# A long convolution with a spectral mix on one core: the last batch's output taken from each half block of u, in groups of four positions by 89 rows

## The chip, the core and the metric

The kernel runs on one core of one Trainium2 chip. TensorE (PE) does the matrix products, its weight loads are shown apart as PEld; ScalarE (ACT) and VectorE (DVE) take results out of the matmul accumulator (PSUM); SyncE (SP) issues the stores. The metric is the device time of one execution in microseconds (us). The trace has its own clock, which starts with the span; all times on that clock are given so.

## The reference, cut to what is computed

For x of 8 batches by 5696 positions by 128 channels and a filter h of 5696 by 128:

```python
L = 2 * S
y = np.fft.irfft(np.fft.rfft(x, n=L, axis=1) * np.fft.rfft(h, n=L, axis=0)[None], n=L, axis=1)[:, :S, :]
X = np.fft.rfft(y, axis=1)                 # 64 lowest modes mixed by w_r + i w_i over the channels
Y[:, :64] = X[:, :64] @ (w_r + 1j * w_i)   # per mode; the other modes are zero
u = y + np.fft.irfft(Y, n=S, axis=1)
out = u + np.maximum(u @ w_ch, 0.0)        # 8 x 5696 x 128, float32
```

## The kernel before, in words

A position s is written s = 64 q + p, with 89 values of q and 64 of p (`J = 64`, `NQ = 89`). The transforms are matmuls with constant tables. The batches go in four pairs (`g_` from 0 to 3). A first stage, up to some 250 us, makes spectra and parks them in a scratch tensor of the device memory; a last stage, in which all that follows lies, brings them back (`load_zt`, L503) and makes the output.

The last stage has two kinds of work.

- `u_tile` (L754) makes u for one batch, eight values of p and all 89 q: 2 matmuls of 356 columns and 16 of 89 columns into two PSUM banks, and one evacuation of 712 elements that writes the tile u transposed, 128 channels by 5696 positions. The evacuation goes to ACT in five cases of eight and to DVE in three. A block is 16 values of p (`ZB`), four blocks (`NCH`) make a batch, so a batch has 8 half blocks.
- `o_tile` (L808) makes 512 outputs per row: four matmuls whose weights are 128 positions of u, taken at a step of `NW` = 44, and whose moving operand is the 256 columns of w_ch and the identity, into two PSUM banks; then ACT makes the relu into one of three R buffers, and DVE adds u and writes an O buffer. A batch of 5696 positions has eleven such tiles of 128 rows by 4 positions and a tail of 64 positions. Two tiles share one O buffer of 1024 columns (`NO8` = 7 buffers) and are stored by one DMA of 128 rows by 4 KB; the eleventh and the tail have small buffers and stores of their own (`Os`).

Both kinds take their two banks from the same four places in turn (`LSLOT`, L722). The order of the work is written out by hand at the end of the function: all engines follow the order in which the code records it, and `Recorder` (L21) puts in the waits. `todo` is a list of o_tiles that are due. After each half block of u some of them are taken from its head. A batch's o_tiles read every position of u at a step of 44, so they come due only when all 8 half blocks of the batch are done.

For the last pair the order is batch 0's four blocks, then batch 1's. At its start 24 o_tiles (of pair 2) are due. After each half block of batch 0 two are taken, after the half blocks of batch 1 two and three in turn; the 12 of batch 0 come due in the middle. When the last half block of u is done, three more o_tiles of batch 0 are taken and then the 12 of batch 1, for which no u work is left. In the last batch tiles 8 to 10 are stored singly (256 KB each).

```python
for half in range(2):
    u_tile(i, b, half)
    for _ in range((2, 2 + half)[n >= NCH] if last else 1 + half):
        if todo:
            o_tile(*todo.pop(0))
```

Every store goes out by `dma("sync", ...)` on SP, in the order of recording, with one of 12 semaphores of the ring `o`; a store waits until the store 12 before it on that ring has landed. SP also issues the loads of the parked spectra; those of the last block are issued at 329.54 us, before pair 3 starts. The loads of x at the start of the kernel (`x_load`, L352) are split into 80 and 9 rows (`QA`, L338), with rows of 4 KB that lie 32 KB apart in memory.

Of the kernel before, what the change touches and what calls it, by code (L numbers as in the profile page):

```python
# [4 lines left out]
P = 128  # L5
# [4 lines left out]
ADD = mybir.AluOpType.add  # L10
# [3 lines left out]
RELU = mybir.ActivationFunctionType.Relu  # L14
# [109 lines left out]
def bass_long_conv_fft__then__afno_spectral_mix_kernel(nc, x, h, moe_w_r, moe_w_i, moe_w_ch, out):  # L124
    B, S, D = x.shape
    M = moe_w_r.shape[0]
    assert D == P and M == 64 and B == 8
    J = 64
    NQ = S // J
# [3 lines left out]
    NP = B // 2  # L133
# [72 lines left out]
    def at(name, cols, dt, off):  # L206
        return nc.alloc_sbuf_tensor_at(name, [P, cols], dt, offset=off)
# [45 lines left out]
    ZB = 16  # L253
# [13 lines left out]
    u_sb = [at(f"UT{i}", S, F16, u_off[i]) for i in range(4)]  # L267
# [3 lines left out]
    NO8, NO = len(o_big), len(o_off)  # L271
    o8_sb = [at(f"O{i}", 1024, F32, o_big[i]) for i in range(NO8)]
    o_sb = [at(f"Os{i}", 512, F32, o_off[i]) for i in range(NO)]
    r_off = [a_g + 16384 + 2048 * i for i in range(3)]
    NR = len(r_off)
    r_sb = [at(f"R{i}", 512, F32, r_off[i]) for i in range(NR)]
# [12 lines left out]
    def pv(bank, off, dims, p0=0, n=P):  # L289
        return bass.AP(ps, p0 * 4096 + bank * 512 + off, [[4096, n]] + [list(d) for d in dims])  # L290

    R = Recorder(nc)
# [3 lines left out]
    def bank(i):  # L296
        return ("bank", i)
# [18 lines left out]
    def dma(eng, dst, src, ring, reads=(), writes=(), after=()):  # L316
        R.add(eng, lambda h_: h_.dma_start(dst, src), reads, writes, ring=ring, after=after)  # L317

    def mm(o, l, r, st, sp, reads, writes):
        R.add("tensor", lambda h_: h_.matmul(o, l, r, start=st, stop=sp), reads, writes)  # L320
# [3 lines left out]
    def once(key, toks):  # L324
        if key in first:
            return []
        first[key] = 1
        return list(toks)
# [3 lines left out]
    def turns(name, items):  # L332
        i = ring2.get(name, 0)
        ring2[name] = i + 1
        return items[i % len(items)]


    QA = 80  # L338
# [59 lines left out]
    W1, W2, WI = wc_sb[:, 0:P], wc_sb[:, P:2 * P], wi_sb[:, :]  # L398
# [17 lines left out]
    for j in range(16):  # L416
        t = turns("h", [0, 2, 4])
# [85 lines left out]
    def load_zt(i, eng="sync", more=()):  # L503
        g_, c_ = divmod(i, J // ZB)
        for part, (p0, r0, n) in enumerate(((0, 0, P), (PB, P, RB))):
            old = list(once(("zt", i % NC, part), zt_old[i % NC][part])) + list(more) + pace
            dma(eng, bass.AP(zt[i % NC][part], p0 * ZP, [[ZP, n], [1, ZP]]),
                bass.AP(zs, (g_ * 2 * NK + r0) * J * 256 + c_ * ZB * 256, [[J * 256, n], [1, ZP]]),
                "q" if eng == "gpsimd" else "t", [("zd", g_, s_) for s_ in range(NT)], [("zt", i % NC, part)], after=old)
# [212 lines left out]
    LSLOT = [0, 2, 4, 6]  # L722
    NCH = J // ZB
# [30 lines left out]
    def u_tile(i, b, half):  # L754
        g_, c_ = divmod(i, NCH)
        t = ahead.get((i, b, half))
        if t is None:
            t = u_z(i, b, half)
        else:
            for hb in range(2):  # L760
                u_c(i, b, half, t, hb, False)
        ub = (g_ % 2) * 2 + b
        old = {0: WT, 1: WT, 2: U_ALL, 3: U_ALL}[ub]
        n_ev[0] += 1
        e = "scalar" if n_ev[0] % 8 in (0, 2, 3, 5, 7) else "vector"
        src = pv(t, 0, [[1, NQ], [512, 2], [NQ, 4]])
        evac(bass.AP(u_sb[ub], c_ * ZB + half * 8, [[S, P], [J, NQ], [4, 2], [1, 4]]),
             src, [bank(t), bank(t + 1)], [("u_", ub, 2 * c_ + half)], eng=e, after=once(("u", ub), old))
# [16 lines left out]
    for hb in range(2):  # L785
        evac(bass.AP(y_sb, hb * 32 * B, [[2 * M * B, P], [B, 32], [M * B, 2], [1, B]]),
             pv(6 + hb, 0, [[2 * B, 32], [B, 2], [1, B]]), [bank(6 + hb)], [("y", hb)], eng="vector" if hb else "scalar",
             after=ZY)
    for b in range(B):
        bk = 6 + b // 4  # L790
# [10 lines left out]
    n_o = [0]  # L801
    o_cur = [0]
    o8_old = [H_ALL] * 2 + [U_ALL] + [G_ALL + ZX] * 2 + [WT] * 2
    o_old = [H_ALL] * 2 + [M_ALL[5:6], U_ALL + [("f1",)]]
    NW = S // P
    TAIL = S - NW * P

    def o_tile(g_, b, r4):  # L808
        ub = (g_ % 2) * 2 + b
        bb = 2 * g_ + b  # L810
        t = turns("l", LSLOT)
        i = n_o[0]
        n_o[0] += 1
        full = r4 < NW // 4
        last_ = (g_, b) == (NP - 1, 1)
        wide = r4 < (8 if last_ else NW // 4 // 2 * 2)
        big = wide or (last_ and full)
        h_ = r4 % 2 if wide else 0
        if big:
            if not h_:  # L820
                o_cur[0] = turns("o8", list(range(NO8)))
            ob, key, old = o8_sb[o_cur[0]], ("o8", o_cur[0]), o8_old[o_cur[0]]
        else:
            k_ = turns("os", list(range(NO)))
            ob, key, old = o_sb[k_], ("os", k_), o_old[k_]
        OW = 1024 if big else 512
        n, rows = (4, P) if full else (1, TAIL)
        rd = [("u_", ub, c_) for c_ in range(2 * NCH)] + [("wch",), ("i16",)]
        for j in range(n):
            lh = bass.AP(u_sb[ub], 4 * r4 + j, [[S, P], [NW, P]]) if full else u_sb[ub][:, NW * P:S]  # L830
            mm(pv(t + j // 2, (j % 2) * 256, [[1, 256]], 0, rows), lh, WI, True, True, rd, [bank(t + j // 2)])
        bk = [bank(t), bank(t + 1)] if full else [bank(t)]
        rs = r_sb[i % NR]
        rv = bass.AP(rs, 0, [[512, rows], [P, n], [1, P]])
        ov = bass.AP(ob, h_ * 512, [[OW, rows], [P, n], [1, P]])
        src_r, src_u = pv(t, 0, [[256, n], [1, P]], 0, rows), pv(t, P, [[256, n], [1, P]], 0, rows)
        R.add("scalar", lambda e: e.activation(rv, src_r, RELU), bk, [("r", i % NR)], after=once(("r", i % NR), G_ALL + XTT + [("y", 0), ("y", 1), ("id",)]))  # L837
        R.add("vector", lambda e: e.tensor_tensor(ov, src_u, rv, ADD), bk + [("r", i % NR)],  # L838
              [key + (h_,)], after=once(key, old))
        if wide and not h_:  # L840
            return
        w_ = (2 if wide else 1) * 4 * D
        if full:
            dst = bass.AP(out.tensor, out.offset + bb * S * D + (4 * r4 - 4 * h_) * D, [[NW * D, P], [1, w_]])
            src = ob[:, 0:w_]
        else:
            dst = bass.AP(out.tensor, out.offset + bb * S * D + NW * P * D, [[D, TAIL], [1, D]])
            src = ob[0:TAIL, 0:P]
        dma("sync", dst, src, "o", [key + (v_,) for v_ in range(h_ + 1)])

    todo = []
    NB = NCH * NP
    NW4 = NW // 4 + 1
    for g_ in range(NP):
        last = g_ == NP - 1
        order = [(c_, b) for b in range(2) for c_ in range(NCH)] if last else [(c_, b) for c_ in range(NCH) for b in range(2)]
        for n, (c_, b) in enumerate(order):
            i = NCH * g_ + c_
            for half in range(2):
                u_tile(i, b, half)  # L860
                for _ in range((2, 2 + half)[n >= NCH] if last else 1 + half):
                    if todo:
                        o_tile(*todo.pop(0))
            if b == 1 and i + NC < NB:
                load_zt(i + NC)
            if last and n == NCH - 1:
                todo += [(g_, 0, r4) for r4 in range(NW4)]
        todo += [(g_, b, r4) for b in range(1 if last else 0, 2) for r4 in range(NW4)]
    while todo:
        o_tile(*todo.pop(0))  # L870
    R.add("sync", lambda e: e.nop(), [], [("o8", i, v_) for i in range(NO8) for v_ in range(2)] + [("os", i, 0) for i in range(NO)])

    R.emit()
# [29 lines left out]
```

## Time and profile before

| what | value |
|---|---|
| median of 3 runs | 380.75 us (380.23 to 383.44) |
| the profiled execution's own time | 383.51 us |
| its span, first to last instruction | 381.7 us |
| mean granted TensorE clock | 0.933 |
| busy share of the span: PE, PEld, DVE, ACT | 95%, 73%, 80%, 82% |
| pair 3 begins (first matmul of its first half block) | 334.04 us |
| last half block of u begins | 365.45 us |
| last DVE instruction ends | 376.48 us |

A timeline line has the start, the duration, the engine, the source line, the operation with out<-in and shape, the count of merged instructions, and in brackets the idle time ahead of it with what ended it. All matmuls have line L320 and all DMAs L317, because helpers record them; they are told apart by the tiles: `ps<-IBs,C` opens a half block of u (twice in each), `ps<-WI,UT` are the matmuls of an o_tile, `UT<-ps` is the evacuation of u, `R<-ps` the relu and `O<-ps,R` the sum. In a table of windows each engine has its busy time and its instructions, then come the granted clock, the busy share of the 16 DMA engines and their rate.

### The profile page before, as it was taken

To read this page: it belongs to the slowest core of one execution; us is meant where nothing else is said; L and a number is where in the kernel's file an instruction comes from. 1 tells how busy PE (TensorE), PEld (TensorE's weight loads), DVE (VectorE), ACT (ScalarE), POOL (GpSimd) and SP (SyncE) were. 2 spreads that over 40 slices of the span, in tenths; PEclk is the share of its full clock that TensorE was granted. 3 is DMA by queue.
4 is the path that set the end of the run, shared out by engine and by line. 5 is a ranking of instruction groups with operands and counts; after the bars stand their busy time and mean duration, and the time that the engine had idled before them with its cause. 6 is when DMAs were issued, how large, how long until landed. Compare 5 with 4: busy or idle time off the path is not lost.

```text
span 381.7 us, 11950 instructions
## 1 busy us (share of the span) xinstructions
PE 363.6 (95%) x5107; PEld 280.4 (73%) x5107; DVE 303.7 (80%) x331; ACT 311.9 (82%) x492; POOL 83.9 (22%) x137
## 2 busy tenths in 40 slices
PE   7998989999989999999999899999999999999992
PEld 4898856667856667766668666668898988888871
DVE  7566998998988998889998888766347766777784
ACT  8357989998989998999998899994466777777783
POOL 8400012320823311822203211339000000000000
PEclk9997999999999999999999999996899999999997
DMA  7998589998999996999996599999999999999867
GB/s 137 201 280 349 140 228 227 276 269 238 107 134 228 234 269 167 143 129 250 235 283 119 137 298 251 300 328 406 407 388 402 402 415 414 404 408 378 342 256 313
DMA packets 84560, 103.92 MB, mean 272 GB/s; under 512 B 22126, under 2 KB 68974, under 8 KB 81538
## 3 DMA queue, kind: packets, MB, share of 16 engines
q1 hardware_dynamic: 59643, 67.73, 51.3%
q0 software_dynamic: 24864, 35.43, 44.3%
q8 instruction: 40, 0.66, 0.7%
q14 instruction: 13, 0.11, 0.1%
HBM read 70.61 MB, written 51.12 MB: 319 GB/s over the span
## 4 chain that ended last, share of the span: by engine, by line
PE 82%; ACT 9%; DVE 6%; issue 1%; DMA 0%; DVEq 0%
PE ps L320 82%; ACT As L310 7%; DVE As L314 2%; DVE U L597 1%; DVE Hs L312 1%; ACT R L837 0%; DMA F<-cF 0%; DVE UT L312 0%; ACT UT L308 0%; ACT XT L310 0%; DVE O L838 0%; PE ps L791 0%; ACT Hs L308 0%; DVE Os L838 0%; ACT Ah L310 0%
## 5 line engine op out<-in xcount | busy, mean ns | idle before, releaser
L320 PE MATMUL ps<-U,Wc 128*128 128x512 f16 (+1 forms) x368 | 95.8, 384 | 0.0
L605 DVE TENSOR_TENSOR U<-Xs,Hs 128x2048 f16<-128x2048 f16 (+1 forms) x68 | 80.7, 1189 | 11.5 <-ACT Xs L308 10.0
L308 ACT CAST Xs<-ps 128x1024 f16<-128x1024 f32 (+1 forms) x72 | 69.5, 971 | 7.8 <-PE ps L320 4.8
L838 DVE TENSOR_TENSOR O<-ps,R 128x512 f32<-128x512 f32 x81 | 52.5, 686 | 19.8 <-ACT R L837 12.5
L308 ACT CAST Zs<-ps 128x512 f16<-128x512 f32 (+1 forms) x126 | 66.0, 604 | 0.0
L837 ACT ACTIVATE R<-ps 128x512 f32<-128x512 f32 x96 | 50.9, 573 | 14.6 <-PE ps L320 14.1
L314 DVE TENSOR_SCALAR As<-ps 128x720 f16<-128x720 f32 (+1 forms) x60 | 50.1, 879 | 9.1 <-PE ps L320 8.0
L310 ACT ACTIVATE As<-ps 128x720 f16<-128x720 f32 (+1 forms) x72 | 51.6, 772 | 6.6 <-PE ps L320 5.7
L320 PE MATMUL ps<-F,Xin 128*128 128x180 f16 x512 | 54.5, 255 | 2.6 <-ACT Ah L310 1.0
L320 PEld LDWEIGHTS ps<-F,Xin 128*128 128x128 f16 x512 | 46.8, 156 | 9.3 <-DVE As L314 2.6
L320 PE MATMUL ps<-WI,UT 128*128 128x256 f16 x360 | 52.5, 281 | 0.5 <-DVE O L838 0.4
L320 PE MATMUL ps<-As,M 64*128 64x128 f16 x1440 | 48.9, 217 | 4.3 <-DVE U L597 3.5
L320 PEld LDWEIGHTS ps<-U,Wc 128*128 128x128 f16 x368 | 28.5, 98 | 28.5 <-ACT Zs L308 6.1
L320 PEld LDWEIGHTS ps<-As,M 64*128 64x128 f16 x1440 | 40.5, 94 | 10.9 <-DVE U L597 4.2
L317 POOL DMA_DIRECT2D Xt<-in_x_dram x48 | 24.8, 520 | 102.9 <-PE ps L320 102.2
L605 DVE TENSOR_TENSOR U<-ps,Hs 128x2048 f16<-128x2048 f32 x20 | 45.7, 2283 | 0.0
L308 ACT CAST UT<-ps 128x712 f16<-128x712 f32 x40 | 30.0, 752 | 18.7 <-PE ps L320 18.7
L320 PEld LDWEIGHTS ps<-WI,UT 128*128 128x128 f16 x360 | 39.5, 152 | 4.4 <-issue 2.2
L320 PE MATMUL ps<-IBs,C 128*128 128x356 f16 x128 | 40.8, 328 | 0.4
L320 PEld LDWEIGHTS ps<-G,Zs 128*128 128x128 f16 x492 | 27.3, 97 | 13.3
L308 ACT CAST Zt<-ps 128x512 f16<-128x512 f32 (+1 forms) x58 | 31.0, 606 | 0.1
L320 PE MATMUL ps<-G,Zs 128*128 128x2 f16 (+2 forms) x492 | 30.5, 192 | 0.0
(88 smaller groups left out, 500.3 us busy)
## 6 DMA issues: line engine op xcount, KB each, us to landing
out_dram<-O SPq DMA_DIRECT2D x39, 512.0 KB, 10.4
zscr<-Zs SPq DMA_DIRECT2D x60, 256.0 KB, 6.3
Xt<-in_x_dram POOLq DMA_DIRECT2D x24, 320.0 KB, 6.9
zscr<-Zt SPq DMA_DIRECT2D x28, 256.0 KB, 6.6
W<-wscr POOLq DMA_DIRECT2D x8, 512.0 KB, 5.3
M<-cM POOLq DMA_DIRECT2D x5, 720.0 KB, 20.3
ZT0a<-zscr SPq DMA_DIRECT2D x3, 1024.0 KB, 13.4
Xr<-in_x_dram POOLq DMA_DIRECT2D x8, 320.0 KB, 13.8
```

What stands on the lines that cost most here:

```text
L308: R.add(e, lambda h_: h_.copy(dst, src), reads, writes, after=after)
L310: R.add(e, lambda h_: h_.activation(dst, src, COPY, scale=scale), reads, writes, after=after)
L312: R.add(e, lambda h_: h_.tensor_copy(dst, src), reads, writes, after=after)
L314: R.add(e, lambda h_: h_.tensor_scalar_mul(dst, src, scale), reads, writes, after=after)
L317: R.add(eng, lambda h_: h_.dma_start(dst, src), reads, writes, ring=ring, after=after)
L320: R.add("tensor", lambda h_: h_.matmul(o, l, r, start=st, stop=sp), reads, writes)
L597: R.add("vector", lambda e, b=b, s_=s_: e.tensor_tensor(bass.AP(u_s[i], b * 512, [[2048, P], [1024, 2], [1, n * D]]), s_, hv, MULT), [tok, ...
L605: R.add("vector", lambda e: e.tensor_tensor(uv, src, hv, MULT), bk + [("h", t, 0), ("h", t, 1, 0), ("h", t, 1, J)], [("u", i)])
L837: R.add("scalar", lambda e: e.activation(rv, src_r, RELU), bk, [("r", i % NR)], after=once(("r", i % NR), G_ALL + XTT + [("y", 0), ("y", 1 ...
L838: R.add("vector", lambda e: e.tensor_tensor(ov, src_u, rv, ADD), bk + [("r", i % NR)], [key + (h_,)], after=once(key, old))
```

## The change

The last batch (batch 1 of pair 3) no longer uses `o_tile`. Each half block of its u yields two new tiles, recorded by `o_last`: tile i takes the four positions p0+4i to p0+4i+3 and, as weights, the 89 values of q at a step of 64, so it reads that half block alone. It has the same four matmuls of 256 columns, the same relu of 512 columns and the same sum, on 89 rows in place of 128. The two tiles of a half block fill one O buffer, which goes out in two stores: 80 rows and 9 rows of 4 KB, 32 KB apart in the output. The last batch so has 16 tiles and 16 stores, where it had 12 tiles and 8 stores.

The order changes with it: three tiles are taken after every half block of pair 3, four after each half of its last block. The 24 tiles of pair 2 are all taken during batch 0's half blocks, batch 0's own 12 during the first two blocks of batch 1, and the new tiles from then on. After the last half block of u six tiles are left, all of the new kind.

```diff
-        last_ = (g_, b) == (NP - 1, 1)
-        wide = r4 < (8 if last_ else NW // 4 // 2 * 2)
-        big = wide or (last_ and full)
+        big = wide = r4 < NW // 4 // 2 * 2
...
+    def o_last(c_, half, i):
+        ub, bb, p0 = 2 * ((NP - 1) % 2) + 1, B - 1, c_ * ZB + half * 8
+        t = turns("l", LSLOT)
+        k_ = n_o[0]
+        n_o[0] += 1
+        if not i:
+            o_cur[0] = turns("o8", list(range(NO8)))
+        ob, key, old = o8_sb[o_cur[0]], ("o8", o_cur[0]), o8_old[o_cur[0]]
+        for j in range(4):
+            mm(pv(t + j // 2, (j % 2) * 256, [[1, 256]], 0, NQ), bass.AP(u_sb[ub], p0 + 4 * i + j, [[S, P], [J, NQ]]), WI, True, True,
+               [("u_", ub, 2 * c_ + half), ("wch",), ("i16",)], [bank(t + j // 2)])
+        bk = [bank(t), bank(t + 1)]
+        rv = bass.AP(r_sb[k_ % NR], 0, [[512, NQ], [P, 4], [1, P]])
+        ov = bass.AP(ob, i * 512, [[1024, NQ], [P, 4], [1, P]])
+        src_r, src_u = pv(t, 0, [[256, 4], [1, P]], 0, NQ), pv(t, P, [[256, 4], [1, P]], 0, NQ)
+        R.add("scalar", lambda e: e.activation(rv, src_r, RELU), bk, [("r", k_ % NR)])
+        R.add("vector", lambda e: e.tensor_tensor(ov, src_u, rv, ADD), bk + [("r", k_ % NR)], [key + (i,)], after=once(key, old))
+        if i:
+            for q0, n in ((0, QA), (QA, NQ - QA)):
+                dma("sync", bass.AP(out.tensor, out.offset + (bb * S + p0 + q0 * J) * D, [[J * D, n], [1, 8 * D]]), ob[q0:q0 + n, :], "o",
+                    [key + (v_,) for v_ in range(2)])
+
+    def o_next():
+        e = todo.pop(0)
+        (o_last if e[0] == "q" else o_tile)(*e[e[0] == "q":])
...
-                for _ in range((2, 2 + half)[n >= NCH] if last else 1 + half):
+                for _ in range(3 + (n == 2 * NCH - 1) if last else 1 + half):
                     if todo:
-                        o_tile(*todo.pop(0))
+                        o_next()
+                if last and b:
+                    todo += [("q", c_, half, v_) for v_ in range(2)]
...
-        todo += [(g_, b, r4) for b in range(1 if last else 0, 2) for r4 in range(NW4)]
+        if not last:
+            todo += [(g_, b, r4) for b in range(2) for r4 in range(NW4)]
     while todo:
-        o_tile(*todo.pop(0))
+        o_next()
```

## The prediction

> **What bounds the kernel now.** I read the table of windows over the last pair first, cut at the begin of the pair, of its second batch, of the last half block of u, of the first tile after it, and at the last DVE instruction.
>
> ```profile
> core 0: us, PE busy (x) PEld busy (x) DVE busy (x) ACT busy (x) POOL busy (x), PEclk, DMA share, GB/s
> 334.04:349.78 15.74, 15.73 (x205) 13.67 (x206) 11.85 (x19) 11.42 (x23) 0.00 (x0) 0.95 0.97 396
> 349.78:365.45 15.67, 15.52 (x192) 13.30 (x192) 12.60 (x20) 11.48 (x22) 0.00 (x0) 0.95 0.82 328
> 365.45:368.84 3.39, 2.94 (x33) 2.27 (x32) 2.13 (x4) 2.94 (x8) 0.00 (x0) 0.95 0.74 302
> 368.84:376.49 7.65, 6.00 (x41) 4.45 (x41) 7.59 (x14) 6.48 (x12) 0.00 (x0) 0.95 0.76 301
> 376.49:381.70 5.21, 0.00 (x0) 0.00 (x0) 0.00 (x0) 0.00 (x0) 0.00 (x0) 0.60 0.73 283
> ```
>
> Three things stand here. Up to 365 PE is full and DVE and ACT have room (12.60 and 11.48 of 15.67). From 368.84 it is DVE that is full (7.59 of 7.65). Then nothing computes for 5.21 us, and only stores drain. The DMA engines, full at the start (0.97), have room from 350 on. Bytes: 396 x 15.74 + 328 x 15.67 + 302 x 3.39 + 301 x 7.65 + 283 x 5.21 make 16.2 MB after 334.04. Four batches of 2.92 MB and the last small stores of pair 1 (0.29 MB) are 11.95, so some 4.2 MB were queued at 334.04.
>
> Next the timeline of PE and of DVE, for the price of a half block of u with its o_tiles.
>
> ```profile
> 360.76 0.32 PE L320 MATMUL ps<-IBs,C 128*128 128x356 f16 x1
> 361.75 1.71 PE L320 MATMUL ps<-WI,UT 128*128 128x256 f16 x12
> 363.54 0.33 PE L320 MATMUL ps<-IBs,C 128*128 128x356 f16 x1
> 364.53 1.08 PE L320 MATMUL ps<-WI,UT 128*128 128x256 f16 x8
> 365.45 0.32 PE L320 MATMUL ps<-IBs,C 128*128 128x356 f16 x1
> ```
>
> ```profile
> 362.59 0.89 DVE L312 CAST UT<-ps 128x712 f16<-128x712 f32 x1
> 363.39 1.88 DVE L838 TENSOR_TENSOR O<-ps,R 128x512 f32<-128x512 f32 x3
> 369.50 6.80 DVE L838 TENSOR_TENSOR O<-ps,R 128x512 f32<-128x512 f32 x11
> 376.21 0.27 DVE L838 TENSOR_TENSOR Os<-ps,R 64x128 f32<-64x128 f32 x1
> ```
>
> From one opening matmul to the next is a half block: with two tiles 1.91 (363.54 to 365.45), of which u takes 0.99 and 8 matmuls 0.92, so 0.115 each. With three tiles 2.78 (360.76 to 363.54) where DVE evacuates u in it; the same view gives 2.60 for another such (356.25 to 358.85, a tail among its tiles) and 2.47 where ACT does it (351.68 to 354.15). The eleven sums of the last batch run one after the other, 0.62 each.
>
> Last the stores: SP's timeline at the end, and the landing of stores on a quiet ring (window 362 to 366).
>
> ```profile
> 371.95 6.19 SPq L317 DMA_DIRECT2D out_dram<-O  x7
> 378.19 0.65 SPq L317 DMA_DIRECT2D out_dram<-Os  x1
> ```
>
> ```profile
> out_dram<-O SPq DMA_DIRECT2D x2, 512.0 KB, 2.9
> ```
>
> The last store is issued at 378.19, 1.7 us after DVE is done, because SP is still issuing the earlier ones; it lands 3.1 later (same view, window 374 to 379), at 381.3, and the span ends 0.4 after that. A quiet store of 524 KB takes 2.9; at some 410 GB/s 1.3 of it is moving, so 1.6 is fixed.
>
> **The change, part by part.**
>
> *Work added.* 64 matmuls in place of 45 for the last batch: 19 x 0.115 = 2.2 us of PE. Relus and sums: 16 of 512 columns in place of 11 and a tail: ACT 5 x 0.557 (6.68 us for 12 in the tail) less 0.27, 2.5; DVE 5 x 0.62 less 0.27, 2.8. That a sum has 89 rows in place of 128 I count as no saving: the columns are the same.
>
> *The weight load at a step of 64.* No row has this step. 128 columns at a step of 130 paced the matmuls of Xin at 106 ns (54.5 us for 512 of 180 columns), 64 columns at that step those of Hp at 60 ns (15.4 us for 256 of 90 columns): 0.83 to 0.94 ns a column, so 89 columns take 74 to 84, hidden by the 115 of the matmul ahead. I take nothing; it costs from 115 ns up (rival E). A gain there is excluded, since the 256 columns pace the matmul.
>
> *Order.* The instruction order of the changed kernel shows six tiles after the last half block of u, where 15 stood. All 16 half blocks carry three tiles or four. Of the 14 with three, six have u on DVE (the choice counts evacuations and does not change): 8 x 2.47 + 6 x 2.69 = 35.9, less 0.6 for two tails not in those rows; two with four at 2.47 + 4 x 0.115 = 2.93. The last half block so begins at 334.04 + 35.3 + 2.9 = 372.3 (365.45 now). Behind it ACT is the limit: evacuation 1.19 after the begin, 0.65, six relus at 0.557, one sum of 0.69: the last sum ends at 378.2, where it is 376.48 now. If every half block went at 2.47 it is 376.9. The tail of 12 tiles at DVE's pace is gone, but its work and 4 tiles more now stretch the half blocks.
>
> *Waits for buffers.* Pair 2's stores come faster onto a ring with 4.2 MB queued. A store issued at 334 to 338 lands 12.6 later by the landing view; an O buffer comes round after seven pairs, about 16.8 tiles, so 16 us at two tiles per 1.91 and 13.9 at three per 2.5, less 1.2 for filling. Price: nothing to 1 us on DVE around 346 to 350. It moves the engines' end, not the stores', as the ring stays full meanwhile; I take nothing.
>
> *The stores.* SP issues 16 for the batch in place of 8; a store took 0.33 to 1.14 to issue here, the latter where the ring was full. Two per pair of tiles fit into the 1.3 to 1.7 us between pairs. The ring's semaphores make a store wait for the one twelve earlier, six pairs or some 9 us back, against 4.7 to land: no wait. What decides is how fast 80 and 9 rows move. No store here has fewer rows than 128, tails aside. The nearest row is the load of x and h at the start, 80 and 9 rows as well, with the same 32 KB between rows; by bytes these fill the ring until 24 us:
>
> ```profile
> 12.00:15.00 3.00, 3.00 (x40) 2.40 (x38) 2.95 (x5) 0.66 (x1) 2.08 (x4) 0.95 1.05 208
> 15.00:18.00 3.00, 3.00 (x56) 3.00 (x56) 2.31 (x4) 1.65 (x3) 0.00 (x0) 0.95 1.10 217
> 18.00:24.00 6.00, 6.00 (x106) 6.00 (x105) 3.40 (x6) 3.29 (x5) 0.00 (x0) 0.95 1.05 211
> ```
>
> The DMA engines are full and move 211 GB/s, half of the 396 to 415 of 128-row traffic. At 211 a pair of tiles (364,544 bytes) takes 1.73 us; at 410 0.89. These are the bounds; I take 1.73, because shape and pitch are the same. Loads are not stores and POOL issued them, so it is a near row, no proof.
>
> The Trainium skill, "SBUF — State Buffer", section "Door 1: The DMA port swizzle", says that partitions 0 to 63 reach only 8 of 16 ports, about 218 GB/s, no more than 32 partitions do. The 208 to 217 above agree in size. By the page alone the first 64 rows take 1.20 us per pair, and by that estimate the stores would keep up with the tiles and the sum would be that of rival B.
>
> *Sum.* All bytes but the last batch's, 13.3 MB at 410, leave the ring at 366.4. The first new pair is ready 3.8 after the begin of the 13th half block (3.8 as from 363.54 to the second sum's end at 367.37): 366.9 to 368.0. I take 367.0, as the ring will hardly be idle before. Then 8 x 1.73 = 13.8, fixed 1.6, end 0.4: 382.8, against a span of 381.7: +1.1. The profiled execution took 383.51, 1.8 more than its span, and lies 2.76 over the median of the three; by its own time the sum is 384.6, carried to the median 380.75 + 1.1 = 381.9.
>
> **Rivals.**
>
> *B, the stores keep up.* If a pair takes under about 1.3 us, the engines decide: last sum 378.2, 0.45 to issue two stores, 2.9, 0.4: 381.9; with 2.47 throughout and 2.6, the shortest landing here, 380.4. Change +0.25 to -1.35, time 379.4 to 381.0, middle 380.4. For it: 410 GB/s elsewhere. Against: 211 for this shape.
>
> *C, the engines mesh better than the rows.* PE alone needs 0.98 + 12 x 0.115 = 2.36 for three tiles; with that the last sum ends near 375.8, the span at 379.2, time 378.2. Against: no three-tile half block went below 2.47.
>
> *D, slower: the new stores fall well below 211.* Between 58 and 61 us, with x loads beside other traffic, the windows show 58, 115 and 158 GB/s at shares of 0.75 to 0.92. At 137 a pair takes 2.66, the span ends at 367.0 + 21.3 + 2.0 = 390.3, time 389.3. It is slower by over 1% from 2.1 us per pair (174 GB/s). Against: those windows hold small packets too.
>
> *E, the step of 64 slows the weight load.* At twice its price, 160 ns, PE gets 64 x 0.045 = 2.9 us longer: last sum 381.1, span 384.8, time 383.9; over 1% from some 180 ns.
>
> That the change does not do what it says is excluded by the instruction order.
>
> **How the numbers follow.** A (stores at 211) 0.45, own range 381.0 to 383.2; B 0.33; C 0.06; D 0.10; E 0.06. The likeliest is A: 381.9. The range takes in A, B, C and the near part of E, 378.2 to 384.8, and leaves out D and the far part of E. A measurement tells about 1% (3.8 us) from no change; A, B and C lie within it. Faster by over 1% has what lies beyond C, 0.03; slower D and most of E, 0.14; within 0.83.
>
> **What would show it.** In the profile after: the last half block of u begins near 372.3 and the last sum ends near 378.2; six tiles lie behind it. The DMA share is near 1 at about 211 GB/s from 367 to the end, with landings growing from pair to pair; landings that stay at 3 to 4 say B. Weight loads of 89 columns with WI matmuls at 0.115 speak against E. Three-tile half blocks much over 2.7, or DVE waiting on stores around 348, would show the sum of the half blocks wrong.

## The result and the profile after

The changed kernel takes 384.17 us (median of 14 runs, 382.52 to 385.81), the kernel before 380.59 (14 runs, 379.15 to 383.44): ratio 1.0092, 95% interval 1.0069 to 1.0115. That is 3.5 us more, clear of noise; the middle of the interval lies just inside the 1% that the prediction called no change, its upper end beyond it.

The profiled execution of the changed kernel has a span of 381.1 us, shorter than the 381.7 of before. The two must not be set against each other as a whole: pair 3 begins at 331.28 in it and at 334.04 in that of before, though nothing ahead of it was changed. Over all profiled executions below the begin lies anywhere from 330.39 to 334.21. So I count from the begin of pair 3: the last sum ends after 45.96 us (before 42.44) and the span after 49.82 (before 47.66).

The end of the changed kernel on PE and on DVE, from their timelines:

```profile
364.49 0.32 PE L320 MATMUL ps<-IBs,C 128*128 128x356 f16 x1
365.47 2.08 PE L320 MATMUL ps<-WI,UT 128*89 128x256 f16 x12
367.39 0.31 PE L320 MATMUL ps<-IBs,C 128*128 128x356 f16 x1
368.37 2.69 PE L320 MATMUL ps<-WI,UT 128*89 128x256 f16 x16
370.90 0.32 PE L320 MATMUL ps<-IBs,C 128*128 128x356 f16 x1
371.88 3.94 PE L320 MATMUL ps<-WI,UT 128*89 128x256 f16 x24
```

```profile
367.04 1.93 DVE L865 TENSOR_TENSOR O<-ps,R 89x512 f32<-89x512 f32 x3 [0.18 <-ACT R L864]
369.93 2.55 DVE L865 TENSOR_TENSOR O<-ps,R 89x512 f32<-89x512 f32 x4 [0.96 <-ACT R L864]
373.44 3.80 DVE L865 TENSOR_TENSOR O<-ps,R 89x512 f32<-89x512 f32 x6 [0.96 <-ACT R L864]
```

The twelve matmuls from 365.47 end at the next opening one at 367.39: 1.92, so 0.160 us each, and sixteen from 368.37 to 370.90 are 0.158 each. The half block with four tiles takes 3.51 (367.39 to 370.90): 0.98 for u and 2.53 for these sixteen, with no wait of PE in it. The number of sums after the last half block is six, and they run at 0.62 as before: a sum of 89 rows is not shorter than one of 128.

The end of the stores (SP's timeline, and the landing in the window 377.4 to 380):

```profile
365.48 12.51 SPq L317 DMA_DIRECT2D out_dram<-O  x16
```

```profile
out_dram<-O SPq DMA_DIRECT2D x1, 320.0 KB, 3.2
out_dram<-O SPq DMA_DIRECT2D x1, 36.0 KB
```

```profile
366.00:369.00 3.00, 3.00 (x33) 2.88 (x32) 2.79 (x5) 2.21 (x4) 0.00 (x0) 1.00 0.62 182
369.00:372.00 3.00, 3.00 (x33) 2.88 (x33) 2.07 (x4) 2.62 (x5) 0.00 (x0) 1.00 0.63 199
377.24:378.50 1.26, 0.00 (x0) 0.00 (x0) 0.00 (x0) 0.00 (x0) 0.00 (x0) 0.98 0.87 270
```

The last windows (rate in the last column, DMA share ahead of it) show the ring with room while the new stores go out, 0.62 and 0.63. The landings stay at 2.7 to 3.2 in all such windows from 364 on: the stores keep up with the tiles. What follows the last sum, the drain, is 3.86 us, where it was 5.22.

### The profile page after: what moved, and what is told of

Read it like the earlier page. It is cut to its first block, busy times and chain, and to the rows that moved or that the text cites. A ratio compares the mean times of both kernels' runs of the same rounds, so it can differ in the third digit from the quotient of the medians.

```text
span 381.1 us, 12009 instructions
## 1 busy us (share of the span) xinstructions
PE 363.9 (95%) x5126; PEld 282.6 (74%) x5126; DVE 306.0 (80%) x335; ACT 313.9 (82%) x496; POOL 84.4 (22%) x137
## 4 chain that ended last, share of the span: by engine, by line
PE 77%; ACT 11%; DVE 7%; DMA 3%; issue 1%; POOL 0%; DVEq 0%
PE ps L320 77%; ACT As L310 7%; DVE As L314 3%; DMA Xt<-in_x_dram 2%; ACT UT L308 1%; DVE U L597 1%; ACT R L835 1%; DVE Hs L312 1%; DVE O L836 1%; DVE UT L312 1%; ACT R L864 0%; DMA F<-cF 0%; ACT XT L310 0%; DVE O L865 0%; DVE U L605 0%
## 5 line engine op out<-in xcount | busy, mean ns | idle before, releaser
L320 PE MATMUL ps<-U,Wc 128*128 128x512 f16 (+1 forms) x368 | 94.4, 376 | 0.3 <-DVE U L605 0.3
L836 DVE TENSOR_TENSOR O<-ps,R 128x512 f32<-128x512 f32 x70 | 45.5, 686 | 17.0 <-ACT R L835 9.8
L320 PE MATMUL ps<-WI,UT 128*128 128x256 f16 (+1 forms) x379 | 55.8, 286 | 0.0
L320 PE MATMUL ps<-F,Xin 128*128 128x180 f16 x512 | 52.8, 250 | 2.8 <-ACT Ah L310 1.0
L835 ACT ACTIVATE R<-ps 128x512 f32<-128x512 f32 x84 | 44.0, 574 | 13.3 <-PE ps L320 13.3
L320 PEld LDWEIGHTS ps<-F,Xin 128*128 128x128 f16 x512 | 45.1, 155 | 9.6 <-DVE As L314 2.7
L320 PEld LDWEIGHTS ps<-WI,UT 128*128 128x128 f16 (+1 forms) x379 | 44.5, 168 | 2.6 <-issue 1.9
```

## The experiments

Ratios are to the kernel before, with 95% intervals. "Last sum" and "end" are counted from the begin of pair 3 in each profiled execution. The difference of two of these ratios has an error of about 0.003, or 1.1 us (0.004 where e1 is one of the two).

| kernel | ratio | last sum | end |
|---|---|---|---|
| before | 1 | 42.44 | 47.66 |
| changed | 1.0092 (1.0069 to 1.0115) | 45.96 | 49.82 |
| e1_contiguous | 1.0088 (1.0054 to 1.0123) | 46.53 | 50.51 |
| e3_order_only | 1.0003 (0.9979 to 1.0027) | 44.94 | 48.40 |
| e4_more_buffers | 1.0057 (1.0037 to 1.0077) | 46.00 | 49.89 |
| e5_order_buffers | 0.9977 (0.9959 to 0.9995) | 43.54 | 47.01 |
| e6_contiguous_buffers | 1.0055 (1.0032 to 1.0078) | 45.15 | 49.24 |
| e7_twelve_tiles | 1.0005 (0.9987 to 1.0024) | 42.89 | 47.42 |
| e8_small_stores_only | 1.0001 (0.9984 to 1.0019) | 45.13 | 47.37 |
| e9_order_spread | 0.9979 (0.9963 to 0.9996) | 42.20 | 46.20 |

The theory after the first look was W: the weight loads, at 0.160 in place of 0.115, cost 64 x 0.045 = 2.9 us, nearly the whole loss. The rivals were the stores (S) and the denser order (O).

**e1_contiguous**: only the last batch's u is laid down with q inside, so that the weights lie side by side.

```diff
+        if (g_, b) == (NP - 1, 1):
+            src = pv(t, 0, [[512, 2], [1, 4 * NQ]])
+            dst = bass.AP(u_sb[ub], (c_ * ZB + half * 8) * NQ, [[S, P], [4 * NQ, 2], [1, 4 * NQ]])
...
-            mm(..., bass.AP(u_sb[ub], p0 + 4 * i + j, [[S, P], [J, NQ]]), WI, ...)
+            mm(..., bass.AP(u_sb[ub], (p0 + 4 * i + j) * NQ, [[S, P], [1, NQ]]), WI, ...)
```

> The changed kernel with one thing undone: for the last batch u is laid down with its 89 values of q side by side, so the new tiles read their weights at a step of 1 in place of 64. Tiles, order and stores stay. Theory W (the weight load at a step of 64 paces the new tiles: 0.160 us per matmul in the trace after, 0.112 for 128 columns at a step of 44): the 64 matmuls go back to about 0.11, PE gets 64 x 0.047 = 3.0 us shorter, the ratio to before falls from 1.009 to 1.000 to 1.003. Theory N (it is the number of weight columns, 89 in place of 128): nothing changes, 1.009. Theory S (the stores of 80 and 9 rows set the end): the matmuls get shorter but the ratio stays at 1.007 or more.

The loads became quick, and the time did not follow. PE's timeline of this run:

```profile
363.10 1.48 PE L320 MATMUL ps<-WI,UT 128*89 128x256 f16 x12
364.41 0.31 PE L320 MATMUL ps<-IBs,C 128*128 128x356 f16 x1
368.37 1.93 PE L320 MATMUL ps<-WI,UT 128*89 128x256 f16 x16
370.74 0.31 PE L320 MATMUL ps<-IBs,C 128*128 128x356 f16 x1 [0.43 <-DVE O L868]
```

Twelve matmuls take 1.31 (363.10 to 364.41), 0.109 each. But the half block with four tiles now ends in a wait for DVE: PE stands 0.43 us until a sum gives back its place in PSUM, and that half block still takes 3.36 us, where it took 3.51. Most of what PE gained there, it waits. N falls, as the matmuls got shorter with 89 columns as before, and W falls as the cause of the whole time. The numbers are those that S forecast; whether the stores are the reason is tested in e8. The same trace had something that was not looked for, on DVE:

```profile
344.42 1.93 DVE L839 TENSOR_TENSOR O<-ps,R 128x512 f32<-128x512 f32 x3 [1.72 <-DMA out_dram<-O]
```

DVE waits 1.72 us until a store has landed and its O buffer is free, and 0.99 at 336 in the same way (put down to PE there; the trace of e3 names the store for both). That is the wait that the prediction priced at up to 1 us and took as nothing. The profiled execution of the changed kernel does not have it, so the last sums of these two traces (46.53 and 45.96) don't show what the loads are worth; e4 and e6 below do.

**e2_bench**: the changed kernel with matmul groups and store groups behind it, nothing taken out.

> The changed kernel with a measurement behind it, so its time is longer by the added part. First groups of 24 matmuls with weights from a finished u tile, n columns at a step of s, with 64 moving columns (128 at 44 and 1; 89 at 44, 1, 8, 16, 32, 62, 63, 64; 64 at 44 and 64) and with 256 (89 at 1, 44, 63, 64; 128 at 44); then groups of eight stores of 4 KB rows into scratch memory: 128 rows at 22 KB pitch, 128 at 32 KB, 80 and 9 at 32 KB, 80 alone, 64 from partition 0, 64 from partition 32. W: 89 columns at 64 take about 160 ns whatever moves, and 63 or 62 about half of that, under the 0.11 of 256 columns. N: all groups of 89 columns take 160 at 256 moving columns, whatever the step. If steps of 8 to 32 are slow too, the cost goes with powers of two. Stores: if the 211 GB/s of the x loads holds for stores, 80 and 9 rows take 1.73 us a pair, 128 rows 1.25 to 1.3 us each; if the rate goes with the ports, 64 rows from partition 32 are faster than 64 from 0.

Times from the start of a group's 24 matmuls to the next marker, per matmul, with 64 moving columns. The granted clock was 0.50 in these groups, except the first (128 at 44: 0.63) and 89 at 44 (0.92):

| columns, step | ns | columns, step | ns |
|---|---|---|---|
| 128, 44 | 62 | 89, 32 | 148 |
| 128, 1 | 54 | 89, 62 | 156 |
| 89, 1 | 76 | 89, 63 | 152 |
| 89, 44 | 163 | 89, 64 | 147 |
| 89, 8 | 160 | 64, 44 | 129 |
| 89, 16 | 162 | 64, 64 | 116 |

The step of 64 is nothing special: 89 columns cost some 150 to 160 ns at every step measured but 1, so W's forecast for 62 and 63 failed, and 128 columns at a step of 44 cost no more than 62. What makes the new load slow is that it is strided and has fewer than 128 columns, both together. With 256 moving columns, at a clock of 1.00, it is 167 (89 at 44), 157 (89 at 63), 154 (89 at 64) and 109 (128 at 44). The group of 89 at 1 with 256 moving columns came out at 200, at a clock of 0.54, so it can't be set beside these; at a clock of 1.00 the same matmul takes 0.109 us in e1, which N did not allow. The Trainium skill, "TensorE: Matmul & The Clock Gate", section "Weight-path perf modes — Fast Weight Load (FWL) and DoubleRow", says that the quick load is on only when there are 128 weights; 109 against 167 at the same step and clock agrees. The Trainium skill, same page, section "LDWEIGHTS (loading the stationary operand)", prices a load at columns / 1.2 ns, an estimate of 74 ns for 89; that agrees with 76 at a step of 1, and not with the strided rows.

The stores in windows inside each group (128 rows at 22 KB pitch, 128 at 32 KB, 80 and 9, 80, 64 from partition 0, 64 from partition 32):

```profile
383.00:391.00 8.00, 8.00 (x60) 7.58 (x61) 0.00 (x0) 0.00 (x0) 0.00 (x0) 0.64 1.03 419
394.00:403.00 9.00, 9.00 (x57) 8.63 (x57) 0.00 (x0) 0.00 (x0) 0.00 (x0) 0.50 1.03 416
407.00:416.00 9.00, 9.00 (x60) 8.23 (x59) 0.00 (x0) 0.00 (x0) 0.00 (x0) 0.50 0.81 254
422.00:428.00 6.00, 6.00 (x33) 5.70 (x32) 0.00 (x0) 0.00 (x0) 0.00 (x0) 0.65 0.96 267
433.00:440.00 7.00, 7.00 (x49) 6.87 (x49) 0.00 (x0) 0.00 (x0) 0.00 (x0) 1.00 0.98 210
444.50:449.00 4.50, 0.00 (x0) 0.00 (x0) 0.00 (x0) 0.00 (x0) 0.00 (x0) 0.74 1.00 409
```

A pitch of 32 KB costs no more than one of 22 KB (416 and 419). The rows' place decides: 64 rows from partition 0 go at 210 GB/s, 64 from partition 32 at 409. The rule on ports that the prediction took from the Trainium skill, "SBUF — State Buffer", section "Door 1: The DMA port swizzle", holds for stores, by these two rows. A pair of 80 and 9 rows goes at 254: 364,544 bytes in 1.43 us, between the 0.89 and the 1.73 of the prediction. As the DMA share is 0.81 in that window, 1.43 is what a pair takes at most.

**e3_order_only**: the kernel before with the new numbers of tiles per half block; the last batch keeps its tiles.

```diff
-                for _ in range((2, 2 + half)[n >= NCH] if last else 1 + half):
+                for _ in range(3 + (n == 2 * NCH - 1) if last else 1 + half):
```

> The kernel before with the new numbers alone: three tiles after each half block of pair 3, four in its last block. The last batch keeps its 128-row tiles and stores, which all lie behind its last half block, as before; four half blocks then have no tile. Theory W: this part costs nothing; 36 tiles in twelve half blocks of 2.55, four half blocks of 1.0 and 12 tiles of 0.62 end some 0.9 us earlier than before: ratio 0.996 to 1.000. Theory O (denser half blocks stall on buffers and engines and that is the loss): 1.004 or more.

1.0003: neither 0.9 us faster nor slower than can be told. The trace has the same waits as e1 (waits from 329 to 352):

```profile
DVE O L838 <- DMA out_dram<-O: 2.8, 2, 1.7
```

So the order would gain about a microsecond and loses it at O buffers whose stores have not landed. That theory (B) and its rival (R), that the wait only moves on, went into the next three.

**e4_more_buffers, e5_order_buffers, e6_contiguous_buffers**: four more O buffers during pair 3, in the place of a scratch load that pair 3 does not use; on the changed kernel, on e3 and on e1.

```diff
+    NX = len(o_big)
+    o_big += [a_as1 + 4 * ZP + 4096 * i for i in range(4)]
...
+        if last:
+            o_turn[:] = ["o8x", list(range(NX, NO8)) + [(ring2["o8"] + k_) % NX for k_ in range(NX)]]
```

> The changed kernel with four more O buffers during pair 3, in the place of a scratch load that pair 3 does not use: eleven in place of seven. Theory B (at three tiles per half block a buffer comes round before its store has landed, and DVE waits: 2.7 us in two waits in the trace of the contiguous variant, 2.8 in that of the order alone): the waits go, the ratio to before falls from 1.009 to 1.002 to 1.006. Theory R (the ring is full then anyway, so the wait only moves to another place): 1.008 or more.

> The order alone, as before, with the four more O buffers. Theory B: the 2.8 us of waits go and the half blocks run at 2.3 to 2.6, so the ratio falls from 1.000 to 0.992 to 0.997, which would be faster than both kernels. Theory R: 1.000, with the time lost at another wait.

> The contiguous variant with the four more O buffers. Theory B: 1.009 falls to 1.001 to 1.004; from this to 1 is what four more tiles on ACT and DVE cost (some 2.4 us) less the shorter drain of the stores. If it stays some 0.8 us under the run with more buffers and a step of 64, that is the part of the weight load that lies on the path.

B holds: 1.0092 to 1.0057, 1.0003 to 0.9977, 1.0088 to 1.0055: 1.0 to 1.3 us each. Each of these steps is about as large as its error, the three together are clear of it. In e5's trace the sums that had waited for stores wait only for ACT and PE:

```profile
335.28 1.89 DVE L841 TENSOR_TENSOR O<-ps,R 128x512 f32<-128x512 f32 x3 [0.65 <-ACT R L840]
343.07 1.89 DVE L841 TENSOR_TENSOR O<-ps,R 128x512 f32<-128x512 f32 x3 [1.21 <-PE ps L322]
```

DVE stands idle at these sums without a late store too, 0.65 and 1.21 us, so 2.7 us of waits cost less than 2.7. The traces of e3 and e5 begin pair 3 at the same time (330.40 and 330.39), and there the last sum comes 1.4 us earlier with the buffers.

The changed kernel's own profiled execution had no such wait, and its time, 382.88, lies 1.3 us under its median. That its other runs have it is what the step from 1.0092 to 1.0057 says; on its own trace it is not shown, and the begin of pair 3, which moves by 3.8 us, could put one run that far under the median as well. e5 is faster than the kernel before by 0.2% and than the changed one by 1.1%, but missed its 0.992 to 0.997, as e6 missed its 1.001 to 1.004.

e4 and e6 differ by the layout of the last batch's u alone (its evacuations take 0.75 us on ACT and 0.89 on DVE in both), and by 0.0002 in ratio: the times can't tell nothing from about 1 us. Their traces, neither of which has a wait for a store, show where the loads matter. These are half blocks 13 to 15 of pair 3 and the stretch from the opening of the 16th to the last sum, in us:

| trace | 13, three tiles | 14, three tiles | 15, four tiles | 16, to the last sum |
|---|---|---|---|---|
| e4, step of 64 | 2.91 | 2.90 | 3.51 | 6.35 |
| e6, contiguous | 2.31 | 2.97 | 3.35 | 6.18 |

The quick loads gain 0.6 us in one half block and little or nothing in the others, 0.85 in all, where 64 x 0.045 = 2.9 had been reckoned. In half block 14 of e6, where DVE evacuates u, twelve quick matmuls still come to 1.92 (365.06 to 366.98), and at the end of 15 PE waits for DVE:

```profile
364.01 0.31 PE L322 MATMUL ps<-IBs,C 128*128 128x356 f16 x1
365.06 1.80 PE L322 MATMUL ps<-WI,UT 128*89 128x256 f16 x12
366.98 0.32 PE L322 MATMUL ps<-IBs,C 128*128 128x356 f16 x1
370.33 0.31 PE L322 MATMUL ps<-IBs,C 128*128 128x356 f16 x1 [0.43 <-DVE O L871]
```

What is left of e6, 1.0055, is the new form of the last batch. Two kernels took it apart.

**e7_twelve_tiles**: e6 with four of the sixteen tiles left out; the stores stay sixteen.

```diff
-        if i:
+        if i or c_ < 2:
...
-                for _ in range(3 + (n == 2 * NCH - 1) if last else 1 + half):
+                for _ in range(3 + (n == 2 * NCH - 1) - (NCH <= n < NCH + 2) if last else 1 + half):
...
-                    todo += [("q", c_, half, v_) for v_ in range(2)]
+                    todo += [("q", c_, half, v_) for v_ in range(1 if c_ < 2 else 2)]
```

> The contiguous variant with more buffers, with the number of the last batch's tiles put back from 16 to 12: in the first four half blocks of that batch the second tile is left out (those positions of the output get old buffer contents; the stores keep their size), and two tiles in place of three are taken in the half blocks of the first two blocks, so that six are still left at the end. Theory T (the four more tiles on ACT and DVE are the price of the change): four half blocks get 0.47 to 0.6 us shorter each, the ratio falls from 1.0055 to 0.999 to 1.001. Theory S (the stores of 80 and 9 rows, or the six last tiles with their drain, are the price): it stays at 1.004 or more.

1.0005, as T said, so the four tiles cost 1.9 us (0.0050 x 380.5, with an error of 1.1). In the traces the four half blocks that lost a tile take 7.86 us in place of 10.13. A tile left out takes its work from PE, ACT and DVE alike, so this run does not say which engine's work it is that pays.

**e8_small_stores_only**: e6 without the stores of 80 rows.

```diff
-            for q0, n in ((0, QA), (QA, NQ - QA)):
+            for q0, n in ((QA, NQ - QA),):
```

> The contiguous variant with more buffers, without the eight stores of 80 rows (most of the last batch's output is left out; the stores of 9 rows stay, so each step of SP keeps its place). Theory S: the stores at 265 GB/s hold up the end; without them the drain falls from 4.1 us after the last sum to about 3 and the ratio from 1.0055 to 1.002 or less. Theory T: only the last store's own moving time goes, 0.5 to 1 us, ratio 1.003 to 1.004.

1.0001, 2.05 us less, as S said and more than T allowed. The trace shows where: the last sum stays (45.13 against 45.15), and from there to the end it is 2.24 us in place of 4.09. The last sums of e6 and of e8 (spans 380.6 and 378.3):

```profile
372.84 3.67 DVE L871 TENSOR_TENSOR O<-ps,R 89x512 f32<-89x512 f32 x6 [0.87 <-PE ps L322]
372.38 3.68 DVE L871 TENSOR_TENSOR O<-ps,R 89x512 f32<-89x512 f32 x6 [0.86 <-PE ps L322]
```

So the stores cost behind the last sum and nowhere ahead of it. Any kernel has to move a last pair, some 0.9 us at 410 GB/s; about 1.1 us of the 2.05 is then the low rate and the queue of the last pairs. That split is worked out, not measured.

**e9_order_spread**: e5 with batch 0's tiles spread over all half blocks of batch 1.

```diff
-                for _ in range(3 + (n == 2 * NCH - 1) if last else 1 + half):
+                for _ in range((3, 1 + half)[n >= NCH] if last else 1 + half):
```

> The order alone with more buffers, but the last pair's first batch spread over the second batch's half blocks: three tiles after each half block of batch 0, then one and two in turn. No half block of u is then without tiles. If the empty half blocks of the order variant cost something (DVE stood 3.3 us there), the ratio falls from 0.998 to 0.993 to 0.997; if PE sets the pace anyway it stays at 0.998.

0.9979, as e5, so the gain to 0.993 to 0.997 did not come. In the trace the last sum comes 1.3 us earlier, and 0.5 of it is given back behind it (4.00 after the last sum against 3.47); the 0.8 us that is left does not show in the times. Both beat the kernel before, by little more than their error, and the changed one.

## Why the prediction was right or wrong, point by point

- *The sum, 381.9.* Measured 384.17: in the range, 2.3 above the sum and above A's own 381.0 to 383.2, and within 1% as forecast. The range and the "within 1%" held by luck as much as by reckoning: the mechanism that was called likeliest, A, was wrong, and the time nearest to the measured one, the 383.9 of rival E, was got from a cost of which only a part came.
- *A: "At 211 a pair of tiles takes 1.73 us ... I take 1.73", and stores that set the end from 367 on.* Wrong. A pair takes 1.43 at most in the bench. The last batch's eight pairs became ready between the first store at 365.5 and the last sum at 377.2, one per 1.7 us on average, the DMA share was 0.62 and 0.63 in place of near 1, and landings did not grow. Rival B was right that the engines decide, not on its time of 380.4. Only the drain pays: e8 says up to 2.05 us, all of it behind the last sum.
- *The weight load, "74 to 84, hidden by the 115 of the matmul ahead. I take nothing."* Wrong: 0.160 per matmul, the very figure of rival E. The rows of Xin and Hp were read as prices of one load per column, at any number of columns; the bench has 62 for 128 columns at a step of 44 and 116 to 129 for 64 columns at 44 and 64. Why Hp's matmuls came every 60 ns is not shown: they write two halves of the output's partitions in turn (the code sets J * r), and a load lasts 214 ns there, so loads overlap, but no run has such pairs, or the step of 130, by itself. E's 2.9 us did not come either: between e4 and e6 it is 0.1 us in the times and 0.85 in the traces, as the engines hand on through the same places in PSUM.
- *The last sum at 44.2 after the begin* (378.2 less 334.04). Measured 45.96. The fourteen half blocks of three took 36.1 (331.28 to 367.39) against 35.3, the four-tile one 3.51 against 2.93, the stretch behind the last opening 6.34 against 5.9. In the trace of the changed kernel the slow loads make 0.5 of the first (e6 takes 35.6) and pace the whole 3.51. "2.47 + 4 x 0.115" would have failed with quick loads as well: e6 takes 3.35, and PE waits there for one of the four places in PSUM, which u and four tiles more than fill.
- *"Waits for buffers ... I take nothing."* Priced too low: 1.0 to 1.3 us in the times, 1.4 at the last sum between e3 and e5. Of the two waits in e1's and e3's traces the later lies 14 us after the begin, in the stretch that was named (346 to 350, 12 to 16 after it), the earlier 6.6 after it, which was not foreseen. The argument that it "moves the engines' end, not the stores'" fell with the stores as the bound.
- *Work added.* ACT 2.5 and DVE 2.8 were worked out for 16 tiles in place of 12; e7 measures 1.9 for four tiles. This was the largest sure loss, and the sum of A did not hold it, as the stores were to set the end.
- *The tail.* Six tiles in place of 15 behind the last half block, and a drain of 3.86 in place of 5.22. The gain is that of the order, not of the new tiles: e3, with the order alone, drains in 3.46.

Put together, a row of runs leads from the kernel before to the changed one. "Times" is the difference of the ratios, each with an error of 0.7 to 1.2 us; "traces" that of the column "end":

| step | times, us | traces, us |
|---|---|---|
| before to e5: the order, with buffers enough | -0.9 | -0.65 |
| e5 to e7: the new form of the last batch, still 12 tiles | +1.1 | +0.41 |
| e7 to e6: four more tiles | +1.9 | +1.82 |
| e6 to e4: weights at a step of 64 | +0.1 | +0.65 |
| e4 to the changed kernel: seven O buffers | +1.3 | -0.07 |
| sum | +3.5 | +2.16 |

Each column adds up by construction, so its sum proves nothing. The traces give nothing for the last step because the changed kernel's profiled execution had no wait for a store; between e5 and e3 the same step is 1.39 in the traces. In the second step the drain grows by 1.06 us, from 3.47 in e5 to 4.53 in e7, beside the 1.1 worked out from e8, while e7's last sum comes 0.65 earlier. The four tiles (1.9 and 1.8) and the waits for buffers (1.3, and 1.4 between e5 and e3) are the losses that times and traces give alike; the drain and the loads are known to about 1 us.

## What to carry to other kernels

Work taken earlier from a tail is paid where it lands: count the units that the new shape adds (16 tiles for 12, because 89 of 128 rows are used) on every engine, and the buffers that must come round sooner. When PE, ACT and DVE hand on through a few PSUM places, a quicker matmul gains only where PE was the one the others waited for (0.85 of 2.9 us here); ask whose release PE waits for next. An output tile on the first 80 partitions was stored at 267 GB/s, where 128 went at 416, so judge it by the drain behind the last instruction, where nothing hides it.

## What the runs showed of the hardware that I had not expected

- A weight load of 89 columns costs 147 to 163 ns at each of seven steps from 8 to 64, twice a contiguous one (76), while 128 columns at a step of 44 cost no more than 62. The strided load is as slow at a granted clock of 0.50 (147 at a step of 64, 64 moving columns) as at 1.00 (154, 256 moving columns).
- 64 rows from partition 32 are stored at 409 GB/s, 64 from partition 0 at 210.
- The begin of pair 3 differs by 3.8 us between profiled executions of kernels with the same code ahead of it. Neither its cause nor a link to the granted clock was found: 334.21 came at a clock of 0.988, 331.28 too.
